# Retention and soft mixture of experts: the first result write on eight DMA engines

## The chip, the cores and the metric

The kernel runs on one core of a Trainium2 chip. The time is the device time of one execution in microseconds (us), the median of 3 runs. Times inside an execution are counted from the start of the profiled span.

## The reference

First a linear attention with decay. For each of 4 batches and 8 heads, 768 steps of a 64 x 64 state:

```
state = gamma[head] * state + outer(k[t], v[t])
y[t]  = scale * q[t] @ state            # scale = 1/sqrt(64)
```

The outputs of the heads stand side by side as x, 3072 tokens of 512 columns (one row for each batch and step). Then a soft mixture of 8 experts with 4 slots each:

```
logits = x @ phi                        # 3072 x 32
slot_in  = softmax(logits, over tokens).T @ x          # 32 x 512
slot_out[e] = relu(slot_in[e] @ w1[e]) @ w2[e]         # w1: 512 x 1024, w2: 1024 x 512
out = softmax(logits, over slots) @ slot_out           # 3072 x 512
```

All of it is float32.

## The kernel before, in words

The order of all instructions on each engine is written out by hand: the order of the statements is the order on the engine, and nothing is planned by a scheduler. All transfers, loads and writes alike, are issued by SyncE (SP), in one queue.

The attention is worked in chunks of 128 steps, two chunks at a time, and the tokens' logits and the sums for the slots are gathered along the way. Meanwhile the weights w1 and w2 come in, in loads of 2 MB (`load_two`, issued on line 177). The last four of these loads hold the last parts of w2.

After the attention come the experts: `hidden` (line 678) multiplies the slots by w1, the loop of line 766 multiplies the result by w2. The 512 output columns are worked in three blocks (`BLOCKS`) of 256, 128 and 128 columns. Each block ends in the generator `finish`, whose steps are fitted between the matmuls of the following block: at each `yield` it hands back to the loop over units of the next block, which goes on with one unit of its matmuls.

In `finish` the expert outputs of the block are spread over the partitions (line 729), and then for each 64 columns of the block's width there is one unit `u` (line 733): four matmuls (line 742), one for each batch, make 128 output columns (on partitions) for 1536 of the 3072 tokens (on the free axis, three chunks of 128 of each batch). ScalarE and VectorE copy the four results of PSUM into the tile `ot` (line 750), and SP writes the tile to `out` (line 753). The output in DRAM is turned, 512 rows (columns of the model) of 3072 tokens, so a write of 128 rows by 1536 tokens is 768 KB in pieces of 6144 bytes, with 12288 bytes from row to row. The host turns it back.

In order there are eleven writes, numbered here one to eleven. Block 0 has four of 768 KB (its units 0 to 3). Block 1 has one of 768 KB, and from `HELD` on a unit is written in two halves of 384 KB, so that two more follow in block 1 and four in block 2. Write one, with rows 0 to 127 and the first 1536 tokens, is the one that the change touches. The first unit of block 0 has the number `(cb, u) == (0, 0)` and is written in one part.

After the last write the core waits for all writes to land (line 841), and the execution ends.

Of the kernel before, what the change touches and what calls it, by code (L numbers as in the profile page):

```python
# [16 lines left out]
B, H, S, D = 4, 8, 768, 64  # L17
C = 128
NC = S // C
NSTEP = B * NC  # L20
NPAIR = H // 2
NTOK = B * S
DM = H * D
# [3 lines left out]
NK = DM // 128  # L27
NFC = FF // 128
HC = C // 2
NPP = NSTEP // 2  # L30
WARM = 4
WM = 1
# [19 lines left out]
MOVES.update({P: [(P - 1, 0, MIX), (P - 1, 1, MIX)] for P in range(3, 8)})  # L52
WITHK = [[i for i in (2 * P, 2 * P + 1) if i not in TURNED and i < NSTEP - B] for P in range(NPP)]
ROWS = [[P for P in range(1, NPP - B // 2) if len(WITHK[P]) == n] for n in range(3)]
KINDS = [n for n in range(3) if ROWS[n]]
# [10 lines left out]
def head_of(half, g):  # L66
    return 2 * g + np.where(g < NPAIR // 2, half, 1 - half)


def constants():  # L70
# [4 lines left out]
    k[:, K_VC:K_VC + H] = g[None, :] ** -float(C)  # L75
    gy = g[head_of(p[:, None] // HC, np.arange(NPAIR)[None, :])]
    k[:, K_YT:K_YT + 64] = (gy[:, :, None] ** (8 * np.arange(16)) / np.sqrt(D)).reshape(128, 64)
# [7 lines left out]
def retention_soft_moe_kernel(  # L85
# [4 lines left out]
    nc = tc.nc  # L90
    xs = dict(zip(KINDS, arrays))
    xw, wone, wtwo, whalf, wl, kq, head, v1, out = arrays[len(KINDS):]
# [12 lines left out]
    def large(pool, n=4096):  # L105
        return pool.tile([128, n], F32, name="b", tag="b")

    def slot():
        return ring.tile([128, 1024], F32, name="r", tag="r")

    def small(name, shape, bufs=1):
        return cpool.tile(shape, F32, name=name, bufs=bufs)

    def bank(name, shape=(128, 512)):
        return ps.tile(list(shape), F32, name=name)
# [27 lines left out]
    def half(r):  # L143
        return slice(r * HC, (r + 1) * HC)

# [51 lines left out]
    def load_behind(P):  # L197
        m = P - (NPP - B // 2)
        t = st[2 * P]["tile"][:, 0:3072]
        nc.sync.dma_start(t, wl[m])  # L200
        take(early[8 + 12 * m:20 + 12 * m], t)
# [4 lines left out]
    def load_pair(P):  # L206
# [9 lines left out]
        if P == 0:  # L216
# [4 lines left out]
            nc.sync.dma_start(t[:, 2560:3072], v1)  # L221
        elif P >= NPP - B // 2:
            m = P - (NPP - B // 2)
            nc.sync.dma_start(t, xw[m])
# [45 lines left out]
    def carry_mm(P):  # L270
        p = pr[P] = {}
        names = (("Y0", "Y1"), ("A1", "S")) if P == NPP - 1 else (("Y0", "Y1"),)
        p["Y"] = [bank(n).rearrange("p (i g t) -> p i g t", i=2, t=C) for pair in names for n in pair]
# [424 lines left out]
    for hf in range(2):  # L698
        for g2 in range(2):
# [14 lines left out]
                    hidden_t(0)  # L714
    assert not weights

    tags = [["sm", "A2", "A0", "A3", "S", "Y1", "Y0"], ["sm", "A2", "Y1", "A3", "S", "A1", "Y1", "A3"],
            ["sm", "A2", "A0", "Y0", "A1", "A3", "S", "Y1"]]
    pend = []

    def finish(cb, op):
        c0, w = BLOCKS[cb]
        os_ = small("os", [128, 256])
        s4 = slot()
        nc.vector.tensor_copy(os_[:, :w], op[:, :w])
        for _ in range(Y1[cb] - 1):
            yield
        rp = bank("Y0")
        nc.tensor.matmul(rp[:, :w], rep, os_[:, :w], start=True, stop=True)
        nc.vector.tensor_copy(s4[:, :w], rp[:, :w])  # L730
        for _ in range(Y2[cb] - 1):
            yield
        for u in range(w // 64):
            m, h = divmod(u, 2)
            if h == 0:
                ots = large(big)
            ot = ots[:, 2048 * h:2048 * h + 12 * C]
            parts = 2 if (cb, u) >= HELD else 1
            cps = []
            for j in range(B):  # L740
                cp = bank(tags[cb][(B * u + j) % len(tags[cb])]).rearrange("p (c t) -> p c t", t=C)[:, 0:3]
                nc.tensor.matmul(cp, s4[32 * j:32 * j + 32, m * 128:(m + 1) * 128],  # L742
                                 cT[32 * j:32 * j + 32, 3 * h:3 * h + 3, :], start=True, stop=True,
                                 skip_group_check=True, tile_position=(32 * j, 0))
                cps.append(cp)
            if (cb, u) == HELD:
                yield
            for p in range(parts):
                for j in range(p * B // parts, (p + 1) * B // parts):
                    (nc.scalar.copy if j % 2 else nc.vector.tensor_copy)(  # L750
                        ot[:, j * 3 * C:(j + 1) * 3 * C].rearrange("p (c t) -> p c t", t=C), cps[j])
                n = 12 * C // parts
                nc.sync.dma_start(out[c0 + m * 128:c0 + (m + 1) * 128, h * 12 * C + p * n:h * 12 * C + (p + 1) * n],
                                  ot[:, p * n:(p + 1) * n])
                if (cb, u, p) == (*HELD, 0):
                    yield
            for _ in range(BURST[cb]):
                yield

    for cb, (c0, w) in enumerate(BLOCKS):  # L760
        op = bank(("A0", "A1")[cb % 2])
        units = ([(g, 4 * hf + f) for hf in range(2) for g in range(2) for f in range(4)] if cb == 0 else
                 [(g, fc) for g in range(2) for fc in range(NFC)])
        for n, (g, fc) in enumerate(units):
            for j in range(4):
                nc.tensor.matmul(op[32 * j:32 * j + 32, :w], hT[fc // 4][:, fc % 4, 4 * g + j, :],  # L766
                                 w2t[4 * g + j, cb, fc], start=(n == 0), stop=(n == len(units) - 1),
                                 skip_group_check=True, tile_position=(0, 32 * j))
            if cb == 0 and n == 2:
                hidden_t(1)  # L770
            for f in pend:
                next(f, None)
        done = finish(cb, op)
        next(done)
        if cb == len(BLOCKS) - 1:
            next(pend[0])
            next(pend[0])
            next(done)
        for f in pend:
            for _ in f:  # L780
                pass
        pend = [done]
# [41 lines left out]
                head=np.concatenate([constants(), phi.reshape(128, NPAIR * NSLOT), vn[0]], axis=1), v1=vn[1])  # L824


_OUT = (DM, NTOK)


# [16 lines left out]
```

## Time and profile before

| | us |
|---|---|
| median of 3 runs (148.18 to 148.61) | 148.55 |
| the profiled execution | 148.68 |
| its span in the profile | 147.0 |
| TensorE busy (matmul) | 136.7 (93%) |
| VectorE busy | 92.5 (63%) |
| ScalarE busy | 77.9 (53%) |
| GpSimd busy | 73.2 (50%) |

The span is the stretch from the first to the last instruction in the profile; the execution's own time is 1.7 us longer. 59.2 MB are moved in 6792 packets, at a mean of 403 GB/s; 52.56 MB are read from DRAM and 6.29 MB written. The core has 16 DMA engines, and a share of DMA time in the views is the mean over these 16: a share of 0.5 can be eight engines that work all the time. The profile does not tell the engines apart by number. A transfer has landed when its last engine is done, and "issue to landing" counts from the start of the instruction on SP to then.

### The profile page before, as it was taken

The numbers are of one execution on the slowest core, as the hardware profiler recorded it, in microseconds if no ns is written. First come the engines' busy times: TensorE is split into PE (matmuls) and PEld (weight loads), VectorE is DVE, ScalarE is ACT, GpSimd is POOL, SyncE is SP. The second block draws the span as 40 slices with busy tenths as digits, with TensorE's granted clock in tenths as the row PEclk, the third lists the DMA queues.
The fourth block names the chain that finished last, engine by engine and source line by source line (L and its number), as shares of the span: only waits on it lengthen the run. The fifth ranks groups of instructions, "written<-read, shape, count | busy, mean of one in ns | idle before, by whom it ended". The sixth has DMA issues, their size and how long they took to land.

```text
span 147.0 us, 5562 instructions
## 1 busy us (share of the span) xinstructions
PE 136.7 (93%) x2378; PEld 101.5 (69%) x2378; DVE 92.5 (63%) x199; ACT 77.9 (53%) x196; POOL 73.2 (50%) x139
## 2 busy tenths in 40 slices
PE   7999999999999999999999989999999999989800
PEld 2678989997999799978988868864333466557400
DVE  0386847977988898979897999486320202563530
ACT  3082496798679875989485795650510100442320
POOL 2035499999979897888693998901100000000000
PEclk9999999999999999999999999999999999999996
DMA  4999999999999999999999999999999999899894
GB/s 169 355 409 422 435 423 436 409 446 416 417 424 404 439 425 430 425 416 436 424 428 424 428 419 417 415 420 409 419 441 430 428 428 419 350 389 380 343 397 168
DMA packets 6792, 59.20 MB, mean 403 GB/s; under 512 B 752, under 2 KB 752, under 8 KB 3440
## 3 DMA queue, kind: packets, MB, share of 16 engines
q1 hardware_dynamic: 6768, 58.85, 96.0%
q8 instruction: 18, 0.29, 0.8%
q14 instruction: 6, 0.05, 0.1%
HBM read 52.56 MB, written 6.29 MB: 400 GB/s over the span
## 4 chain that ended last, share of the span: by engine, by line
PE 82%; DVE 7%; DMA 4%; issue 1%; SPq 1%; DVEq 0%; POOL 0%
PE Y L292 15%; PE A L259 14%; PE A L766 9%; PE S L321 6%; PE Y L283 6%; PE Y L678 5%; PE A L678 5%; PE A L235 5%; DMA r<-in_head_dram 4%; PE sm L375 3%; PE Y L431 2%; DVE b L750 2%; PE sm L742 2%; DVE r L267 2%; PE Y L235 1%; PE S L742 1%
## 5 line engine op out<-in xcount | busy, mean ns | idle before, releaser
L358 ACT COPY r<-r 32x256 f32<-32x256 f32 x96 | 38.6, 402 | 5.7 <-DVE r L348 4.7
L267 DVE TENSOR_TENSOR r<-A,mi 128x512 f32<-128x512 f32 (+1 forms) x50 | 30.1, 661 | 11.7 <-PE A L259 11.7
L358 POOL COPY r<-r 32x256 f32<-32x256 f32 x64 | 25.2, 393 | 6.0 <-DVE r L348 2.0
L259 PE MATMUL A<-b 64*128 64x128 f32 x384 | 25.2, 279 | 0.3 <-DMA b<-in_kq_dram 0.2
L259 PEld LDWEIGHTS A<-b 64*128 64x128 f32 x384 | 22.6, 188 | 3.5 <-issue 1.5
L248 POOL TENSOR_TENSOR b<-b,kt 128x512 f32<-128x512 f32 x22 | 22.5, 1043 | 2.4 <-ACT kt L508 2.0
L292 PE MATMUL Y<-r,b 128*64 128x128 f32 x352 | 22.5, 276 | 0.7 <-DVE r L267 0.5
L292 PEld LDWEIGHTS Y<-r,b 128*64 128x64 f32 x352 | 19.2, 137 | 3.1 <-issue 1.2
L241 POOL TENSOR_TENSOR b<-b,qtab 128x256 f32<-128x256 f32 x20 | 14.3, 738 | 6.9 <-DMA b<-in_x_dram 4.4
L766 PE MATMUL A<-b,r 128*32 128x128 f32 (+1 forms) x368 | 15.7, 307 | 0.0
L766 PEld LDWEIGHTS A<-b,r 128*32 128x32 f32 x368 | 10.6, 110 | 5.8 <-issue 3.8
L750 ACT COPY b<-A 128x384 f32<-128x384 f32 x10 | 4.5, 483 | 16.8 <-PE A L742 15.2
L348 DVE STREAM_TRANSPOSE r<-r 128x1024 f32<-128x1024 f32 x10 | 12.4, 1237 | 0.0
L283 PE MATMUL Y<-b,sst 64*64 64x128 f32 x304 | 10.6, 276 | 0.0
L321 PE MATMUL S<-b 128*64 128x64 f32 x304 | 10.5, 222 | 0.0
L321 PEld LDWEIGHTS S<-b 128*64 128x64 f32 x304 | 10.2, 138 | 0.0
L236 ACT COPY b<-A 128x512 f32<-128x512 f32 x13 | 7.2, 588 | 4.4 <-PE A L235 4.0
L283 PEld LDWEIGHTS Y<-b,sst 64*64 64x64 f32 x304 | 8.2, 133 | 1.3 <-issue 0.2
L312 DVE TENSOR_TENSOR r<-Y,qtab 128x512 f32<-128x512 f32 x9 | 6.2, 692 | 4.2 <-PE Y L292 4.2
L235 PE MATMUL A<-mi,b 128*128 128x128 f32 x52 | 7.6, 281 | 0.0
L375 PEld LDWEIGHTS sm<-r,kt 128*32 128x32 f32 x192 | 5.3, 110 | 2.8 <-issue 2.7
L678 PE MATMUL A<-b,qtab 128*32 128x512 f32 x64 | 7.1, 594 | 0.0
(159 smaller groups left out, 189.5 us busy)
## 6 DMA issues: line engine op xcount, KB each, us to landing
b<-in_wtwo_dram SPq DMA_DIRECT2D x12, 2048.0 KB, 16.1
b<-in_x_dram SPq DMA_DIRECT2D x8, 1536.0 KB, 10.7
b<-in_xw_dram SPq DMA_DIRECT2D x2, 2048.0 KB, 14.5
out_dram<-b SPq DMA_DIRECT2D x5, 768.0 KB, 6.6
b<-in_wl_dram SPq DMA_DIRECT2D x2, 1536.0 KB, 11.5
out_dram<-b SPq DMA_DIRECT2D x6, 384.0 KB, 3.9
b<-in_wone_dram SPq DMA_DIRECT2D x2, 1024.0 KB, 12.1
b<-in_x_dram SPq DMA_DIRECT2D x2, 768.0 KB, 8.3
```

The costliest lines, as they stand in the source:

```text
L235: nc.tensor.transpose(kp[:, g * 128:(g + 1) * 128], st[i]["kT"][:, g, :], ident)
L241: nc.gpsimd.tensor_tensor(q[:, 0:2], q[:, 0:2], qtab[:, 0:2], ALU.mult)
L248: nc.gpsimd.tensor_tensor(v, v, vsc[:, a:b].unsqueeze(2).broadcast_to([128, b - a, D]), ALU.mult)
L259: nc.tensor.matmul(s["sc"][r][:, g, :], s["kT"][half(r), g, :], s["qT"][half(r), g, :], start=True, stop=True, skip_group_check=True)
L267: nc.vector.tensor_tensor(s["A"][:, r, g:g + n], s["sc"][r][:, g:g + n], mask.unsqueeze(1).broadcast_to([128, n, C]), ALU.mult)
L283: nc.tensor.matmul(p["y"][k][b][half(half_of(r, g)), gl, :], sst[(2 * P + k) % B][half(r), g, :], s["qT"][half(r), g, :], start=(gl == 0 a ...
L292: nc.tensor.matmul(pr[P]["y"][k][g // 2][half(half_of(r, g)), g % 2, :], s["v"][:, 2 * g + r, :], s["A"][:, r, g, :], start=(P < B // 2 an ...
L321: nc.tensor.matmul(S_[half(r), k, g, :], s["kn"][:, 2 * g + r, :], s["v"][:, 2 * g + r, :], start=True, stop=True, skip_group_check=True)
L348: nc.vector.transpose(x, pr[P]["yT"].rearrange("p i g t -> p (i g t)"))
L358: {"s": nc.scalar.copy, "g": nc.gpsimd.tensor_copy}[on[n % len(on)]](xn[32 * b:32 * b + 32, :, a], x[32 * a:32 * a + 32, :, b])
L678: nc.tensor.matmul(hp[hf][32 * j:32 * j + 32, :], si0[:, a:a + NSLOT], w1t[hf, g, k][j], start=(g == 0 and k == 0), stop=(g == 1 and k == ...
L766: nc.tensor.matmul(op[32 * j:32 * j + 32, :w], hT[fc // 4][:, fc % 4, 4 * g + j, :], w2t[4 * g + j, cb, fc], start=(n == 0), stop=(n == le ...
```

## The change

Write one is no longer one transfer of 128 partitions into rows 0 to 127 of `out`. It is four transfers of 32 partitions each (`q` from 0 to 3), 192 KB, into an area of DRAM behind the 512 rows. This area (`gaps`) has 4 x 8 x 5 rows of 1536 elements. Each transfer fills, in each of eight blocks of five rows, the first four rows; the fifth stays empty. Within a block the four rows of 6144 bytes follow each other without space. The output tensor has 80 more rows of 3072 for it. On the host the area's rows are copied to their place before the output is turned.

The `continue` ends the unit's only part. It passes a `yield` that belongs to another unit, `HELD`. The other ten writes are as before.

```
+GAP = (4, 8, 5)
...
+    gaps = out[DM:].rearrange("r t -> (r t)").rearrange("(q a b t) -> q a b t", q=GAP[0], a=GAP[1], b=GAP[2])
...
                 n = 12 * C // parts
+                if (cb, u) == (0, 0):
+                    for q in range(GAP[0]):
+                        nc.sync.dma_start(gaps[q, :, 0:GAP[2] - 1], ot[32 * q:32 * q + 32, 0:n])
+                    continue
                 nc.sync.dma_start(out[c0 + m * 128:c0 + (m + 1) * 128, h * 12 * C + p * n:h * 12 * C + (p + 1) * n],
                                   ot[:, p * n:(p + 1) * n])
...
-_OUT = (DM, NTOK)
+_OUT = (DM + int(np.prod(GAP)) // 2, NTOK)
...
-    o = np.asarray(r.results[0]["out_0_dram"]).reshape(DM, 2, B, NC // 2, C)
+    o = np.array(r.results[0]["out_0_dram"])
+    o[0:C, 0:NTOK // 2] = o[DM:].reshape(*GAP, NTOK // 2)[:, :, 0:-1].reshape(C, NTOK // 2)
+    o = o[0:DM].reshape(DM, 2, B, NC // 2, C)
```

## Rows read from the trace of the kernel before

**Rows 1.** The page: engines' busy time, DMA queues, the chain's share by engine.

```profile
PE 136.7 (93%) x2378; PEld 101.5 (69%) x2378; DVE 92.5 (63%) x199; ACT 77.9 (53%) x196; POOL 73.2 (50%) x139
...
q1 hardware_dynamic: 6768, 58.85, 96.0%
q8 instruction: 18, 0.29, 0.8%
...
PE 82%; DVE 7%; DMA 4%; issue 1%; SPq 1%; DVEq 0%; POOL 0%
```

**Rows 2.** Chain of waits, its last piece: start, length, what.

```profile
140.54 0.47 DVE b L750
```

**Rows 3.** SP's queue in order of time: last load; writes one, two, four, five, eleven.

```profile
108.40 0.33 SPq L177 DMA_DIRECT2D b<-in_wtwo_dram  x1
...
126.74 0.35 SPq L753 DMA_DIRECT2D out_dram<-b  x1
128.39 0.34 SPq L753 DMA_DIRECT2D out_dram<-b  x1
...
131.70 0.33 SPq L753 DMA_DIRECT2D out_dram<-b  x1
135.82 0.33 SPq L753 DMA_DIRECT2D out_dram<-b  x1
...
141.43 0.91 SPq L753 DMA_DIRECT2D out_dram<-b  x1
```

**Rows 4.** Issue to landing, one transfer each: last load; writes four, five, six, eleven.

```profile
DMA to landing us min/median/max: 22.9/22.9/22.9
...
DMA to landing us min/median/max: 6.9/6.9/6.9
DMA to landing us min/median/max: 4.6/4.6/4.6
DMA to landing us min/median/max: 3.5/3.5/3.5
...
DMA to landing us min/median/max: 4.7/4.7/4.7
```

**Rows 5.** Stretches from write one to the end; last columns: PE clock, DMA share, GB/s.

```profile
126.75:127.50 0.75, 0.75 (x20) 0.29 (x16) 0.20 (x1) 0.15 (x1) 0.00 (x0) 1.00 0.51 218
...
130.00:132.00 2.00, 1.81 (x48) 1.09 (x41) 1.22 (x3) 0.86 (x2) 0.00 (x0) 1.00 1.00 412
135.00:135.25 0.25, 0.25 (x16) 0.25 (x12) 0.25 (x1) 0.24 (x1) 0.00 (x0) 1.00 0.68 270
135.25:135.50 0.25, 0.25 (x20) 0.25 (x16) 0.11 (x1) 0.00 (x0) 0.00 (x0) 1.00 0.53 221
135.75:136.00 0.25, 0.25 (x18) 0.25 (x12) 0.00 (x0) 0.00 (x0) 0.00 (x0) 1.00 0.59 246
136.25:136.50 0.25, 0.25 (x12) 0.15 (x8) 0.01 (x1) 0.00 (x0) 0.00 (x0) 1.00 0.43 156
142.00:144.00 2.00, 0.00 (x0) 0.00 (x0) 0.00 (x0) 0.00 (x0) 0.00 (x0) 1.00 1.01 401
144.75:145.00 0.25, 0.00 (x0) 0.00 (x0) 0.00 (x0) 0.00 (x0) 0.00 (x0) 0.50 0.20 74
...
145.25:145.50 0.25, 0.00 (x0) 0.00 (x0) 0.00 (x0) 0.00 (x0) 0.00 (x0) 0.50 0.09 37
145.50:145.75 0.25, 0.00 (x0) 0.00 (x0) 0.00 (x0) 0.00 (x0) 0.00 (x0) 0.50 0.06 25
```

**Rows 6.** DMA packets begun in 127.57:127.65, 136.63:136.72 and 136.72:136.81 (writes: under 8 KB).

```profile
DMA packets 7, 0.05 MB, mean 666 GB/s; under 512 B 0, under 2 KB 0, under 8 KB 6
...
DMA packets 8, 0.05 MB, mean 546 GB/s; under 512 B 0, under 2 KB 0, under 8 KB 8
DMA packets 5, 0.03 MB, mean 341 GB/s; under 512 B 0, under 2 KB 0, under 8 KB 5
```

**Rows 7.** SP's queue: two loads issued one behind the other.

```profile
94.60 0.90 SPq L188 DMA_DIRECT2D r<-in_whalf_dram  x2
```

## The prediction

> **What bounds the kernel now.** I read the page's totals first, then the chain of waits, then the end stretch by stretch, since the change touches one write in the last seventh of the span. TensorE is busy 93% of the span and holds 82% of the chain, while the transfers that SP issues take 96% of sixteen DMA engines' time [rows 1]. Both are full; the question is which of them sets the last microseconds. The chain's last piece is a VectorE copy at 140.54 to 141.01 [rows 2], after which no engine computes; the last write is issued at 141.43 [rows 3] and lands 4.7 us later, at 146.1 [rows 4]. The span is 147.0, so 0.9 us of closing waits follow the landing. From 141.0 on the time is thus DMA time alone.
>
> What the reader should see there is that the sixteen DMA engines do not end together. The windows' DMA share times 16 is the number of engines at work. In 142 to 144 it is 1.01: all of them. From 144.75 to 145.00 it is 0.20, three engines; from 145.25 to 145.50 0.09, one to two; up to 145.75 0.06, one [rows 5]. So thirteen engines end near 144.75 and three end 0.4 to 1.0 us later, and these three set the time.
>
> They are late since the loads. The last load of weights is issued at 108.40 [rows 3] and lands 22.9 us later [rows 4], at 131.3, but already in 126.75 to 127.50 the share is 0.51 [rows 5]: eight engines have finished it and stand idle, eight are still reading, up to 4 us longer. A cause fits in size: the instruction fetches, 18 packets of 16 KB in 0.8% of sixteen engines' 147 us [rows 1], are 0.008 x 16 x 147 = 18.8 us, about 1.05 us for each fetch on one engine; eight late engines with two or three fetches each are late by about what is seen. The first write is issued at 126.74 [rows 3], so it finds eight engines free and eight with a backlog; six packets of its size start between 127.57 and 127.65 [rows 6], some 0.85 us after the issue.
>
> **The change part by part.** *The moved bytes.* 768 KB on sixteen engines are 48 KB each. All sixteen move 412 GB/s in 130 to 132 [rows 5], 25.8 GB/s for one, so 48 KB take 1.9 us. On eight engines each has 96 KB, 3.8 us: eight engines gain 1.9 us of work and eight lose 1.9 us. The total is the same; only who does it changes.
>
> *The relieved eight,* if these are the late ones. Between write four and write five there is a pause: write five is issued at 135.82 [rows 3] and its data start some 0.85 us later, near 136.7: of thirteen packets of its size, eight begin between 136.63 and 136.72 and five up to 136.81 [rows 6]. Write four, issued at 131.70 [rows 3], lands 6.9 us later [rows 4], at 138.6; 1.9 us earlier it would land at 136.7, its engine being done 0.35 us before that (the last write's engine ends at 145.75 and lands at 146.1), so before write five starts. All late engines would catch up there, and the floor of the end is that of the thirteen: 1.0 us earlier.
>
> *The loaded eight,* if these are the early ones. Their pause before write five pays for the extra work, and no more than that. The share falls to 0.68 in 135.00 to 135.25, 0.53 in the next quarter, 0.59 in 135.75 to 136.00 and 0.43 in 136.25 to 136.50 [rows 5]: five engines are free at about 135.1, seven to eight by 135.5, and the last of the eight perhaps by 136. Their pause up to 136.7 is 1.6 us for the first and 0.7 us or less for the last, against 1.9 us of extra work. So they begin write five 0.3 us late at best and about 1.2 us late at worst. How much of a lateness survives to the end is read from today's late engines: write five lands 4.6 us after its issue [rows 4], at 140.4, where an engine with no backlog would need 0.85 + 1.9 + 0.35 for the landing, 138.9; they are 1.5 us late there and 1.0 us at the end, so some 0.5 us is made up. A lateness of 0.3 to 1.2 us becomes 0 to 0.7, or up to 1.2 if none is made up. Against the 1.0 us of today the gain is 0.2 us less than nothing to 1.0 us; the last of the eight decides, since one engine is enough to hold the end. I take 0.65 us late at the end, a gain of 0.35, nearest to the row of 136.25 to 136.50, where the last of them comes free.
>
> *The three added issues.* Two loads issued one behind the other take 0.90 us of SP's queue [rows 7], 0.45 us each, so four issues run from 126.74 to about 128.5. Write two, issued at 128.39, slips by 0.1 to 0.2 us. Nothing but later writes is queued behind it on SP, and every engine has work until then or later: the early eight to 131.4 with the doubled write, the late eight with loads to 129 and more; so I cost it at nothing, and at 0.2 us for the relieved engines if that cover fails, which their pause before write five absorbs. The `continue` passes no yield (the one behind it is for another unit), so TensorE's order stays. The copies before the write are unchanged. Three more completions on an engine cannot gain; above they are bounded by what write six's landing of 3.5 us [rows 4] has over 0.85 + 0.95 + 0.35 us, 1.35, nearly all of it backlog of the write before; I take nothing. The gap in DRAM moves no bytes, and no row before shows a write of this row order; I bound it at 10% of 3.8 us either way, -0.4 to +0.4 us, and take 0.
>
> [...]
>
> *Sum.* The profiled execution took 148.68 us, span 147.0 and 1.7 us around it; less 0.35 that is 148.33. The median of the runs is 148.55, which makes 148.2.
>
> **The rivals.** *The eight are the wrong ones.* The rows count engines but do not name them. If the new writes run on engines that are late, the last engine gets 1.9 us more with no pause to take it up (it works from the load to the end): 148.55 + 1.8 = 150.3 to 150.5. It decides as soon as one of the three late ones is among the eight. By the share alone it would be even odds. What speaks against it is the order of starts: on write five thirteen waiting engines begin over 0.18 us, eight of them in the first half; on write one, where only early engines wait, six begin in 0.08 us and none of them as late after the issue as the last five of write five [rows 6]. So the early engines look like those that are served first, the low end of the order, and a transfer cut to eight engines would most simply take these; it is indirect. [...] Chance 0.16.
>
> *It doesn't do what it says.* The four writes still go over all sixteen engines, or over engines chosen afresh for each: then bytes and engines are as before, only three issues more, 148.55, at most 0.2 above. Every transfer in this trace has 128 partitions, so none shows how blocks of eight are spread. Chance 0.09.
>
> *The early eight become the last.* Same mechanism as the forecast, but one slow engine of the eight keeps the full lateness of 1.0 us or more: 148.45 to 148.75, no change. This is the forecast's upper end and is counted with it.
>
> **How the numbers follow.** The forecast, early eight loaded, has 0.75; its own range is 147.7 to 148.7. This kernel's runs can tell a change only beyond 0.3%, 0.45 us, that is below 148.1 or above 149.0. The forecast's gain lies between 0 and 0.9 around 0.35, so its 0.75 is split 0.37 faster, 0.33 same and 0.05 slower. Without effect 0.08 same, 0.01 slower; the wrong eight 0.16 slower. Together faster 0.37, same 0.41, slower 0.22. The range of 147.6 to 149.0 leaves out the wrong eight and little else.
>
> **What would show it.** In the changed trace: four issues of 192 KB from 126.7 to 128.5; the share in the end's quarters falling within 0.5 us instead of 1.0; write four landing in less than 6.9 us; the pause before write five gone for eight engines (share at 135.25 to 136.50 near 0.5 to 0.6, though from the other half); TensorE's times unchanged up to 141. Wrong if write one's parts land late (over 5 us for the first of them), which would mean that they queue behind the loads, or if the tail has engines that end 2 us after the rest.

## The result, and the profile after

The changed kernel takes 149.99 us (median of 6 runs, 149.16 to 150.91) against 148.56 us (6 runs, 148.18 to 148.62) for the kernel before: the ratio is 1.01, with a 95% interval of 1.0061 to 1.014. It is slower by 1.4 us, where 0.35 us of gain were forecast. The profiled execution took 149.87 us with a span of 148.2, so 1.19 us more than that of before. All ratios are taken from undisturbed runs alone and are not ratios of the medians, which take in every run; where the two differ the ratio counts.

From the page of the changed kernel: busy times, DMA queues, the chain's shares by engine. They answer to [rows 1].

```profile
PE 137.2 (93%) x2378; PEld 102.0 (69%) x2378; DVE 92.3 (62%) x199; ACT 77.9 (53%) x196; POOL 73.4 (50%) x139
...
q1 hardware_dynamic: 6784, 58.85, 95.7%
q8 instruction: 18, 0.29, 0.8%
...
PE 87%; DVE 4%; DMA 2%; issue 0%; DVEq 0%
```

The totals hardly move: same bytes, same matmuls. The 1.2 us are not in the totals but in which engine works when. The last VectorE copy of the changed kernel (start, length) is over at 140.59, 0.4 us earlier than [rows 2]; so the computation is not what got slower.

```profile
140.04 0.55 DVE L752 COPY b<-S 128x384 f32<-128x384 f32 x1
```

SP's queue of the changed kernel, start and length: last load, writes two, five and eleven, which answer to [rows 3]. Line 757 issues the four parts of write one, line 759 the other writes.

```profile
108.22 0.33 SPq L178 DMA_DIRECT2D b<-in_wtwo_dram  x1
...
129.66 0.36 SPq L759 DMA_DIRECT2D out_dram<-b  x1
...
135.01 0.33 SPq L759 DMA_DIRECT2D out_dram<-b  x1
...
142.23 0.73 SPq L759 DMA_DIRECT2D out_dram<-b  x1
```

The four parts by themselves, in the view of one source line (shortest, median and longest duration in ns, first and last start):

```profile
L757 SPq DMA_DIRECT2D out_dram<-b x4: 652/672/821, 126.6 to 128.9; - x4
```

One issue of this form takes 0.65 to 0.82 us where the one of before took 0.35 [rows 3]. Four of them hold SP from 126.56 to 129.54. The last load went out 0.18 us earlier than before, so without the change write two would have gone at 128.21; it goes at 129.66, 1.45 us late.

Issue to landing of writes four, five and eleven, against 6.9, 4.6 and 4.7 us in [rows 4]:

```profile
DMA to landing us min/median/max: 8.0/8.0/8.0
DMA to landing us min/median/max: 6.5/6.5/6.5
...
DMA to landing us min/median/max: 4.9/4.9/4.9
```

Did the parts run on the engines that were free? DMA packets begun between 127.85 and 128.10, some 1.4 us after the first issue (under 8 KB are writes):

```profile
DMA packets 10, 0.10 MB, mean 410 GB/s; under 512 B 0, under 2 KB 0, under 8 KB 6
```

Six writing packets begin together, while other engines still begin load packets. So six of the eight engines were free ones, as read from [rows 6].

The other two were not. The trace also records each count of a transfer's semaphore with its time: sixteen for each transfer of before, the last of them at the landing. Each of the four parts has nine. The first comes 1.1 to 1.2 us after the issue, for the first part before any data start; the other eight are read as the landings on eight engines, as sixteen counts go with sixteen engines. For the first part they fall at 129.25 to 129.32 on six engines and at 130.41 and 130.60 on the last two. These two began more than 1 us later: by its own counts the last load of weights reaches eight engines by 128.08 and the next ones only at 129.14, 129.33 and later.

The stretches of the changed kernel; the last two columns are the DMA share and GB/s. They answer to [rows 5].

```profile
126.50:131.50 5.00, 5.00 (x112) 2.84 (x104) 3.12 (x7) 2.58 (x6) 0.00 (x0) 1.00 0.68 252
...
129.50:130.00 0.50, 0.50 (x12) 0.29 (x8) 0.30 (x1) 0.18 (x1) 0.00 (x0) 1.00 0.46 123
130.00:130.50 0.50, 0.50 (x16) 0.16 (x12) 0.07 (x1) 0.03 (x1) 0.00 (x0) 1.00 0.48 197
...
131.50:132.00 0.50, 0.35 (x10) 0.24 (x2) 0.15 (x1) 0.00 (x0) 0.00 (x0) 1.00 1.38 295
...
135.00:137.50 2.50, 2.28 (x50) 1.34 (x38) 0.91 (x3) 0.58 (x2) 0.00 (x0) 1.00 1.03 410
...
145.00:145.25 0.25, 0.00 (x0) 0.00 (x0) 0.00 (x0) 0.00 (x0) 0.00 (x0) 0.50 0.91 356
145.25:145.50 0.25, 0.00 (x0) 0.00 (x0) 0.00 (x0) 0.00 (x0) 0.00 (x0) 0.50 0.58 234
...
146.50:146.75 0.25, 0.00 (x0) 0.00 (x0) 0.00 (x0) 0.00 (x0) 0.00 (x0) 0.50 0.09 37
146.75:147.00 0.25, 0.00 (x0) 0.00 (x0) 0.00 (x0) 0.00 (x0) 0.00 (x0) 0.50 0.00 0
```

The kernel before in two of these stretches, and its last full quarter:

```profile
126.50:131.50 5.00, 5.00 (x108) 2.97 (x112) 3.11 (x7) 2.63 (x7) 0.00 (x0) 1.00 0.92 377
...
135.00:137.50 2.50, 2.50 (x62) 1.76 (x54) 0.85 (x3) 0.40 (x2) 0.00 (x0) 1.00 0.70 280
...
144.50:144.75 0.25, 0.00 (x0) 0.00 (x0) 0.00 (x0) 0.00 (x0) 0.00 (x0) 0.50 0.84 320
```

Three things are to be seen. First, between 126.5 and 131.5 the share falls from 0.92 to 0.68: 0.24 x 16 x 5.0 = 19 engine-microseconds without work, 1.2 us for each engine. Around 130 half of the engines stand idle: most of the eight without a part of write one (the relieved ones) have finished their loads, and write two is not there yet. Second, the pause before write five, 0.30 x 16 x 2.5 = 12 engine-microseconds before, is gone for all sixteen, not for eight. Third, the end: the first engines finish about 0.5 us later (the share is 0.91 up to 145.25, before 0.84 up to 144.75), and the last one 1.0 us later (146.75 against 145.75). The spread of the end, 1.0 us before, has become 1.5 us. Such ends are those of one execution each, and executions of one kernel differ by some 0.5 us and more, so a spread is a sign and not a price.

### The profile page after: what moved, and what is told of

Same layout as the page of the kernel before. It is cut to its first block, busy times and chain, and to the rows that moved or that the text cites. A ratio compares the mean times of both kernels' runs of the same rounds, so it can differ in the third digit from the quotient of the medians.

```text
span 148.2 us, 5565 instructions
## 1 busy us (share of the span) xinstructions
PE 137.2 (93%) x2378; PEld 102.0 (69%) x2378; DVE 92.3 (62%) x199; ACT 77.9 (53%) x196; POOL 73.4 (50%) x139
## 4 chain that ended last, share of the span: by engine, by line
PE 87%; DVE 4%; DMA 2%; issue 0%; DVEq 0%
PE A L260 17%; PE Y L293 14%; PE A L772 9%; PE S L322 6%; PE Y L284 6%; PE Y L679 5%; PE A L679 5%; PE A L236 5%; PE sm L376 4%; PE Y L432 3%; DMA b<-in_kq_dram 2%; DVE b L752 2%; PE sm L744 2%; DVE r L268 2%; PE Y L236 1%; PE S L744 1%
## 5 line engine op out<-in xcount | busy, mean ns | idle before, releaser
L260 PE MATMUL A<-b 64*128 64x128 f32 x384 | 25.7, 282 | 0.1
```

Source lines behind the costliest of these rows:

```text
L260: nc.tensor.matmul(s["sc"][r][:, g, :], s["kT"][half(r), g, :], s["qT"][half(r), g, :], start=True, stop=True, skip_group_check=True)
```

## The experiments

Three theories were set against each other. A: the four long issues hold SP, write two goes late, and the relieved engines idle. B: eight engines read partitions that other engines read at the same time for the next write, and the two slow each other's packets (an assumption of the author: no trace shows which engine reads which partitions). C: the loaded engines carry 1.9 us more than their pause before write five pays for, and the end waits for the last of them. The kernel before ran beside each batch, at 148.49 to 148.69 us. The diffs are against the changed kernel.

**Order of issue.** Write two goes first, the parts of write one behind it.

```
-                    for q in range(GAP[0]):
-                        nc.sync.dma_start(gaps[q, :, 0:GAP[2] - 1], ot[32 * q:32 * q + 32, 0:n])
                     continue
...
+                if (cb, u) == (0, 1):
+                    for q in range(GAP[0]):
+                        nc.sync.dma_start(gaps[q, :, 0:GAP[2] - 1], ots[32 * q:32 * q + 32, 0:n])
```

> Write two is issued first, and the four parts of write one behind it; bytes and engines as in the changed kernel. Theory A (the four issues hold SP's queue for 3 us, so that write two is issued 1.4 us late and the relieved eight stand idle from 129.3 to 130.8): write two goes out at about 128.2, its packets on the relieved eight start at 129.1, no idle stretch, and the time falls by 1 us or more, to 148.3 to 149.0. Theory C (the loaded eight simply have 1.9 us more than their pause pays for): the same 150.0. Theory B (two engines read from the same partitions' side and both slow down): in between, 149.3 to 149.8, since the parts still meet another write.

Measured: 151.06 us, ratio 1.0137 (1.0073 to 1.02). No better. Its stretch of 132 to 133 shows where the idle time went:

```profile
132.00:133.00 1.00, 1.00 (x20) 0.39 (x16) 0.00 (x0) 0.00 (x0) 0.00 (x0) 1.00 0.45 172
```

Now it is write three, issued at 131.37 behind the four parts, for which half of the engines wait. Moving the hold does not remove it.

**Four plain writes.** Four issues of 32 partitions, but to the old rows, meant for all sixteen engines.

```
-                        nc.sync.dma_start(gaps[q, :, 0:GAP[2] - 1], ot[32 * q:32 * q + 32, 0:n])
+                        nc.sync.dma_start(out[32 * q:32 * q + 32, 0:n], ot[32 * q:32 * q + 32, 0:n])
```

> Write one as four writes of 32 partitions to its old rows, without blocks and gaps, so that sixteen engines should move each. Tells the number of issues from the eight engines. If an issue costs 0.35 to 0.45 us here, write two slips by 0.2 us at most and the time is that of before, 148.5 to 148.8: then the 0.65 to 0.82 us of an issue in the changed kernel come from the eight engines. If each issue takes 0.65 us or more here too, the count alone holds the queue and the time is 149.0 to 149.6.

Measured: 149.0 us, ratio 1.0023 (1.0002 to 1.0044). The four issues:

```profile
L757 SPq DMA_DIRECT2D out_dram<-b x4: 361/418/1604, 125.7 to 127.1; - x4
```

Three of them take 0.36 to 0.43 us, so the 0.65 to 0.82 us of the change belong to its form and not to the number of issues. But the fourth takes 1.60 us, and write two goes out as late as in the change, at 128.84 after a first part at 125.75 (3.1 us). It costs 0.3 us: a late write two is cheap here, where the engines have work meanwhile (a DMA share of 0.93 between 126.5 and 131.5, against 0.68 in the change).

**One write on eight engines.** All 128 partitions in one issue, in eight blocks.

```
-GAP = (4, 8, 5)
+GAP = (1, 8, 17)
...
-                    for q in range(GAP[0]):
-                        nc.sync.dma_start(gaps[q, :, 0:GAP[2] - 1], ot[32 * q:32 * q + 32, 0:n])
+                    nc.sync.dma_start(gaps[0, :, 0:GAP[2] - 1], ot[:, 0:n])
```

> Write one as one write of 128 partitions whose rows in DRAM stand in eight blocks of sixteen with gaps: eight engines, one issue. Theory A: SP is held for under 1 us, write two goes out by 128.2 to 128.4, and the time is 148.2 to 148.8, at or under before. Theory C: 149.8 to 150.2 as in the changed kernel, since the same engines get the same bytes. Theory B: 149 to 150, since the engines read partitions that other engines read for write two.

Measured: 153.52 us, ratio 1.0313 (1.0266 to 1.036), with a single issue of 0.77 us. The slowest of all has the shortest hold of those with eight blocks, so A alone can't explain the loss. (That it uses eight engines like the parts of the change is assumed from its form.) Its stretch of 130 to 131 has a full share at a low rate:

```profile
130.00:131.00 1.00, 1.00 (x19) 0.40 (x16) 0.37 (x2) 0.25 (x1) 0.00 (x0) 1.00 0.91 276
```

0.91 of sixteen engines' time is taken, but 276 GB/s are moved where [rows 5] has 412 at 1.00: packets here take longer for the same bytes, as B expects. That shared partitions are the cause no run shows.

**Write one left out.** The four parts are not issued at all; their rows of the output are missing.

```
-                    for q in range(GAP[0]):
-                        nc.sync.dma_start(gaps[q, :, 0:GAP[2] - 1], ot[32 * q:32 * q + 32, 0:n])
                     continue
```

> Write one is left out, all else as before: no bytes of it on any engine. It gives the most that relieving the late engines can bring. If the end is set by three engines with a backlog since the loads, 147.5 to 147.8 (1.0 us or less under before, the span between thirteen and the last engine). If the backlog has little to do with it, 148.2 or more.

Measured: 148.28 us, ratio 0.9967 (0.9944 to 0.999). This bounds the whole idea: with write one costing nothing to anybody, the kernel gains 0.5 us by the ratio and 0.3 by the median, not the 1.0 us of the prediction's floor.

**Halves.** Only the parts with partitions 0 to 63 are written, or only those with 64 to 127; the rest of write one is left out.

```
-                    for q in range(GAP[0]):
+                    for q in (0, 1):
```

> Of the four parts of write one only the first two go out (partitions 0 to 63); partitions 64 to 127 are left out. [...] Theory A (hold of SP's queue): two issues of 0.7 us, write two 0.7 to 0.9 us late, 148.4 to 148.9. Theory C (0.95 us more on eight engines, inside their pause): 148.2 to 148.5. [...]

```
-                    for q in range(GAP[0]):
+                    for q in (2, 3):
```

> The same with the last two parts only (partitions 64 to 127); partitions 0 to 63 are left out. Same issues, bytes and engines as with the lower half. Theories A and C: the same time as the lower half within 0.3 us. Theory B: packets of 450 ns and more between 129 and 132, and 0.4 us or more above the lower half, 148.8 to 149.6.

Measured: 148.38 us, ratio 0.9967 (0.9937 to 0.9997), and 148.15 us, ratio 0.9971 (0.9946 to 0.9996). Both are as fast as with no write at all: the eight carry the 48 KB each that they carried before, and the others none. But the upper half's packets are slow; its stretch of 129.5 to 130:

```profile
129.50:130.00 0.50, 0.50 (x12) 0.31 (x8) 0.43 (x1) 0.31 (x1) 0.00 (x0) 1.00 1.46 315
```

A share above 1 at 315 GB/s: packets overlap and take longer for their bytes. The slow packets that B expects are there, and with half the load they cost nothing that the runs can tell.

**Lower half twice.** The load and the issues of the change, but all parts read partitions 0 to 63, so no packet comes from the upper ones (the upper half's data are not written).

```
-                        nc.sync.dma_start(gaps[q, :, 0:GAP[2] - 1], ot[32 * q:32 * q + 32, 0:n])
+                        nc.sync.dma_start(gaps[q, :, 0:GAP[2] - 1], ot[32 * (q % 2):32 * (q % 2) + 32, 0:n])
```

> Four issues on eight engines as in the changed kernel, but parts three and four read partitions 0 to 63 again in place of 64 to 127. Bytes, issues, engines and rows in DRAM as in the changed kernel. Theories A and C: 150.0 as the changed kernel, within 0.4. Theory B: no packets over 300 ns between 131 and 132, DMA rate of 400 GB/s there instead of 295 to 320, and 149.3 or less.

Measured: 149.99 us, ratio 1.0088 (1.0067 to 1.011): the whole loss without the slow packets of the upper half. Its stretches:

```profile
126.50:131.50 5.00, 5.00 (x112) 2.84 (x104) 3.15 (x7) 2.58 (x6) 0.00 (x0) 1.00 0.68 277
...
144.50:144.75 0.25, 0.00 (x0) 0.00 (x0) 0.00 (x0) 0.00 (x0) 0.00 (x0) 0.50 0.74 295
...
146.75:147.00 0.25, 0.00 (x0) 0.00 (x0) 0.00 (x0) 0.00 (x0) 0.00 (x0) 0.50 0.06 25
```

Without slow packets the first engines end near 144.7, as before, but the last one at 147.0: the spread grows to 2.3 us. The total is that of the change all the same: what the first engines gain, the last ones lose.

**At the pause.** Write one is plain again; write five goes in four parts of the new form instead, when most engines are free.

```
-                if (cb, u) == (0, 0):
+                if (cb, u) == (1, 0):
...
-    o[0:C, 0:NTOK // 2] = o[DM:].reshape(*GAP, NTOK // 2)[:, :, 0:-1].reshape(C, NTOK // 2)
+    o[256:256 + C, 0:NTOK // 2] = o[DM:].reshape(*GAP, NTOK // 2)[:, :, 0:-1].reshape(C, NTOK // 2)
```

> Write one as before; instead write five, issued when most engines are idle, goes out as four parts on eight engines. Shows what an issue costs when the queues are empty. If 0.65 to 0.85 us are the price of an issue of this form, all four take that here too; if it is a wait for full queues, the first ones take 0.35 to 0.45 us. The time: eight engines get 1.9 us more with no pause behind it, 150.0 to 150.8 by theory C alone; 151 or more if shared partitions slow the upper parts too.

Measured: 150.27 us, ratio 1.011 (1.0087 to 1.0133). The four issues and two of its stretches:

```profile
L757 SPq DMA_DIRECT2D out_dram<-b x4: 651/668/816, 135.6 to 137.9; - x4
```

```profile
136.50:137.00 0.50, 0.50 (x8) 0.00 (x0) 0.09 (x1) 0.00 (x0) 0.00 (x0) 1.00 0.23 74
...
138.00:139.00 1.00, 1.00 (x15) 0.64 (x16) 0.46 (x2) 0.10 (x2) 0.00 (x0) 1.00 0.53 160
```

A share near 0.53 while hardly anything else is in flight is eight engines (0.53 x 16 = 8.5), and each part again has eight landings: the form does confine these transfers to eight. The second issue runs from 136.50 to 137.17, while only a quarter of the engines work (0.23), and takes just as long. So the 0.65 to 0.82 us belong to the form and not to a full queue.

**The hold without the load.** Each part carries 128 columns of 1536; the rest of write one is left out.

```
-                        nc.sync.dma_start(gaps[q, :, 0:GAP[2] - 1], ot[32 * q:32 * q + 32, 0:n])
+                        nc.sync.dma_start(gaps[q, :, 0:GAP[2] - 1, 0:C], ot[32 * q:32 * q + 32, 0:C])
```

> The four writes keep their form, their place and their partitions, but each carries 128 columns of 1536 only (16 KB in place of 192 KB); the rest of write one is left out. This keeps SP's four issues (0.65 to 0.82 us each) and the lateness of write two (about 1.45 us) and takes the load off the eight. Theory A (the issues hold the queue, the relieved eight fall idle and that decides): 149.3 to 150.0, nearly that of the change. Theory C (the eight carry 1.9 us more than their pause pays for, and the last engine is one of them): the lateness of write two is covered by the pause before write five, so 148.1 to 148.5, like the kernel with write one left out (148.28).

Measured: 148.06 us, ratio 0.9963 (0.9934 to 0.9993). SP is held as in the change,

```profile
L757 SPq DMA_DIRECT2D out_dram<-b x4: 651/670/821, 125.0 to 127.3; - x4
```

and nothing is lost against leaving write one out. The hold alone is not the cause, as C expected. (The bytes it leaves out widen the pause that covers the hold, so this doesn't clear the hold where the bytes are there.)

**The load without the hold.** Two issues, each of 32 partitions by 3072 columns of a weight tile in place of write one's data. The expectation says 64 partitions for each; as written the two read partitions 0 to 63 together, so this run is no test of B.

```
-GAP = (4, 8, 5)
+GAP = (2, 8, 9)
...
+        wide.append(t)
...
-                        nc.sync.dma_start(gaps[q, :, 0:GAP[2] - 1], ot[32 * q:32 * q + 32, 0:n])
+                        nc.sync.dma_start(gaps[q, :, 0:GAP[2] - 1], wide[9][32 * q:32 * q + 32, 0:2 * n])
```

> Two issues in place of four: each takes 64 partitions by 3072 columns from a weight tile (the output is not write one's data), so each of the eight engines still gets 96 KB, in the same two halves of the partitions as the lower-half-twice kernel spreads them, with half the holding of SP's queue. Theory A: write two goes out about 0.7 us after the write of before instead of 1.45, and the time falls by half of the change's loss or more, to 149.0 to 149.4. Theory C: the eight have the same load and the time stays at 149.8 to 150.3. Theory B (two engines that read the same partitions' side slow each other): the second issue reads the upper 64 partitions as in the change, so its packets take 430 to 700 ns; as the runs so far show it alone costs nothing.

Measured: 149.46 us, ratio 1.0063 (1.0029 to 1.0097). The run isolates the load better than planned. Its data need no copy, so both issues go out at 120.7, long before write two, which is on time:

```profile
120.72 1.55 SPq L760 DMA_DIRECT2D out_dram<-b  x2
128.35 0.35 SPq L762 DMA_DIRECT2D out_dram<-b  x1
```

Its stretches:

```profile
126.50:131.50 5.00, 5.00 (x110) 2.97 (x112) 3.11 (x7) 2.60 (x7) 0.00 (x0) 1.00 0.91 376
...
135.00:137.50 2.50, 2.42 (x54) 1.49 (x43) 0.85 (x4) 0.44 (x2) 0.00 (x0) 1.00 0.82 333
...
144.25:144.50 0.25, 0.00 (x0) 0.00 (x0) 0.00 (x0) 0.00 (x0) 0.00 (x0) 0.50 0.80 307
...
146.00:146.25 0.25, 0.00 (x0) 0.00 (x0) 0.00 (x0) 0.00 (x0) 0.00 (x0) 0.50 0.03 12
```

No idle time (0.91 against 0.92), no late write two, and the kernel is still 0.9 us slower (0.0063 x 148.5; 0.4 to 1.4 by the interval). The first engines end some 0.2 us earlier than before, near 144.45, the last near 146.15: a spread of 1.7 us. This is C by itself. Issue to landing of write five, which was issued at 135.19:

```profile
DMA to landing us min/median/max: 5.7/5.7/5.7
```

The landings on the single engines show who comes last. Part one lands on five of the eight by 129.78, and on the other three at 130.88, 131.40 and 131.75. These three then have no pause at all: each further 48 KB takes them 1.7 to 1.9 us, through write four (138.19, 138.71, 139.04) to write five (140.02, 140.54, 140.88). At the end three engines stand last with the same distances, at 145.67, 146.18 and 146.52; the other thirteen have landed by 145.12.

**Half on eight, half plain.** The lower 64 partitions as two parts, the upper 64 as one plain write.

```
-GAP = (4, 8, 5)
+GAP = (2, 8, 5)
...
+                    nc.sync.dma_start(out[64:C, 0:n], ot[64:C, 0:n])
...
-    o[0:C, 0:NTOK // 2] = o[DM:].reshape(*GAP, NTOK // 2)[:, :, 0:-1].reshape(C, NTOK // 2)
+    o[0:64, 0:NTOK // 2] = o[DM:].reshape(*GAP, NTOK // 2)[:, :, 0:-1].reshape(64, NTOK // 2)
```

> Only the lower 64 partitions go over eight engines, in two issues; the upper 64 are one plain write on all sixteen. The eight get 72 KB instead of 48 (0.95 us more), the others 24 KB instead of 48. Theory C: half the extra load fits the eight's pause of 0.7 to 1.6 us for most of them, so the time is between before and the change, 148.3 to 149.0. Theory A: three issues of .82, .65 and about .4 us, write two about 1.0 us late: 149.3 to 149.7. Theory B: no packet of the upper half is slow, so all of B's share of the loss goes: 148.3 to 148.8.

Measured: 149.65 us, ratio 1.0051 (1.0024 to 1.0078). Half the extra load (72 KB on each of the eight, if the plain half is spread evenly over sixteen) costs about half the loss; that is somewhat more than C forecast from the pause. A's forecast fits the time, though write two was only 0.6 us late (128.39, that is 2.28 us after the first part, where [rows 3] has 1.65 between writes one and two). So neither dose of the extra load gains, and which theory it speaks for stays open.

**Upper half first.** The four parts in reversed order.

```
-                    for q in range(GAP[0]):
+                    for q in reversed(range(GAP[0])):
```

> The four writes in reversed order, the upper partitions first. Load, issues and bytes are those of the change. Theories A and C: 149.7 to 150.3, no difference from the change. Theory B: the slow packets fall into the time when only six to eight engines work, and the first parts land later (about 2 us each instead of 1.1) while the last go at full pace; the time moves by 0.3 us or more, to either side.

Measured: 150.83 us, ratio 1.0141 (1.0091 to 1.0191), an interval that overlaps with that of the change. Whether the order matters stays unclear.

**A longer pause.** The change with write three left out, and the kernel before with the same write left out, so that every engine's pause is some 1.9 us longer (48 KB at 25.8 GB/s, a sixteenth of the 412 in [rows 5]). The same edit in both:

```
+                if (cb, u) == (0, 2):
+                    continue
                 nc.sync.dma_start(out[c0 + m * 128:c0 + (m + 1) * 128, h * 12 * C + p * n:h * 12 * C + (p + 1) * n],
```

> The change with write three (768 KB on all sixteen engines, 1.9 us of each) left out, so every engine's pause before write five is 1.9 us longer. Theory C (the pause is too short for 1.9 us more): now it suffices, the loaded eight begin write five with the others, and the late write two is covered as well: 148.0 to 148.5, within 0.3 us of the kernel before with the same write left out. Rival (the eight lose time that no pause pays, after write five too): 149.2 to 149.9, 1 us or more above it.

> The kernel before with write three left out, to stand beside the change with write three left out. All late engines catch up before write five, as with write one left out (148.28): 148.0 to 148.4 by either theory.

Measured: the change 0.9962 (0.9934 to 0.9991) of the kernel before, that of before 0.9976 (0.9953 to 0.9998). The difference of 1% that the change makes is gone. The change's stretches with the longer pause:

```profile
126.50:131.50 5.00, 4.84 (x109) 3.06 (x106) 3.26 (x7) 2.58 (x6) 0.00 (x0) 1.00 0.79 284
...
143.50:143.75 0.25, 0.00 (x0) 0.00 (x0) 0.00 (x0) 0.00 (x0) 0.00 (x0) 0.50 1.04 406
...
144.00:144.25 0.25, 0.00 (x0) 0.00 (x0) 0.00 (x0) 0.00 (x0) 0.00 (x0) 0.50 0.19 74
144.25:144.50 0.25, 0.00 (x0) 0.00 (x0) 0.00 (x0) 0.00 (x0) 0.00 (x0) 0.50 0.00 0
```

The four long issues, the slow packets and the eight loaded engines are all there; only the pause is longer. The engines end within 0.5 us (1.04 up to 143.75, none after 144.25). This profiled execution took 147.39 us, 1.2 less than the median of its kernel (148.56; 148.26 for the other), so the ratios carry more than its end does. By their intervals, some 0.5 us either way between the two, a long enough pause pays for what the change adds, and the loss is a matter of the pause.

**Two issues at the place.** The load and partitions of the kernel that writes the lower half twice, in two issues that read their 32 partitions twice (the upper half's data are not written).

```
-GAP = (4, 8, 5)
+GAP = (2, 8, 9)
...
-                        nc.sync.dma_start(gaps[q, :, 0:GAP[2] - 1], ot[32 * q:32 * q + 32, 0:n])
+                        src = ot[32 * q:32 * q + 32, 0:n].unsqueeze(1).broadcast_to([32, 2, n])
+                        nc.sync.dma_start(gaps[q, :, 0:GAP[2] - 1], src)
```

> The bytes, engines and partitions of the kernel that writes the lower half twice (each of the eight gets 96 KB, no packets from the upper partitions), at write one's place, but in two issues that read their 32 partitions twice, so SP is held some 1.5 us instead of 3.0 (the upper 64 rows of write one's block get no data of their own). Theory A for the rest of the loss (the holding adds to the load's price): write two at about 128.3 to 128.5, little idle time of the relieved eight, 149.3 to 149.7. Theory C alone: 149.8 to 150.2, as with four issues.

Measured: 150.09 us, ratio 1.0075 (1.0045 to 1.0105). Write two is on time (128.33) and the loss is that of four issues. Its end:

```profile
144.25:144.50 0.25, 0.00 (x0) 0.00 (x0) 0.00 (x0) 0.00 (x0) 0.00 (x0) 0.50 0.78 307
...
147.25:147.50 0.25, 0.00 (x0) 0.00 (x0) 0.00 (x0) 0.00 (x0) 0.00 (x0) 0.50 0.06 25
```

The first engines end near 144.45, the last one at 147.5 or later: 3 us of spread, in an execution of 150.86 us that is 0.8 us above the median. With the hold halved the whole loss is in the late engines.

## Why the prediction was wrong

*The mechanism* was half right. The form takes eight engines (eight landings for each part), six of them in the change were free ones, the bytes and the computation stay as they were, and the pause before write five is what has to pay. That blocks of eight would confine a write to eight engines was shown by no row of before, though the sum rests on it; the changed kernel's eight landings for each part showed it, and a share of 0.53 at the pause agrees.

*The step that failed* is the condition of the loaded eight, "if these are the early ones". It was put at 0.75 and gave all eight a pause of 1.6 to 0.7 us. Not all of the eight are early: two of them in the change and three in the kernel with the load alone were still reading weights when the others began, and the three had no pause at all. The pause of the early ones was read well. In the prediction's reckoning an engine without backlog lands write five 3.1 us after its issue, and the loaded ones were to be 0.3 to 1.2 us late there. With the load alone, where write five could land at 138.29, the five early ones of the eight are at most 1.1 us late (139.37), and at most 0.4 behind the first engine at the end. The three others are 1.7 to 2.6 us late there, and they are the last at the end. (In the change the two late ones stand out less: the last part lands on them at 133.16 and 133.35, on the six at 132.73 to 132.96, and slow packets and fetches, below, lie over the rest.) So the term "0.65 us late at the end" measured 1.7 us with the load alone and 1.5 in the change, where the last engine lands write five 3.4 us late (6.5 against 3.1), against 1.0 at the end of before: a loss, instead of a gain of 0.35. The kernel's time says the same, 0.9 and 1.4 us more. The rival of the wrong eight, with a chance of 0.16, was thus right for two or three of the eight; its price of 150.3 to 150.5 is a little above the 149.99 measured.

The prediction had a row that warned of it: it read eight free engines from a share of 0.51, where [rows 6] shows six packets beginning together. And that a share counts engines without naming them it said itself.

*Instruction fetches* may widen the end in both kernels. One falls into the stretch before write five; DMA queues of the kernel before in 135.3 to 137.0,

```profile
q8 instruction: 1, 0.02, 3.6%
```

and of the changed one in 135.7 to 137.1 (queue, packets, MB, share):

```profile
q8 instruction: 1, 0.02, 4.2%
```

Each takes about 1.0 us of one engine (0.042 x 16 x 1.4 is 0.94). In the kernel before, a packet of write four ends at 136.11, the fetch begins just there, and the packet behind it takes 627 ns where 234 are usual: the engine lands write four at 138.40. It is one of the three that are late from write four on, so these were not all "late since the loads". In the change the fetch begins at 136.09, again followed by a packet of 627 ns, and a smaller one of 8 KB at 135.80. Two engines land write four there at 139.58 and 139.75, the others by 138.82, and two stand last at the end, at 147.12 and 147.17, the others by 146.32. So in the change's own profile the last 0.8 us fit fetches that fell on engines without a pause, and the load by itself fits the seven engines that end 0.3 to 0.8 us behind the first seven. Which engine a fetch hits is inferred from the times of the packets; no run took a fetch away.

*The floor,* a gain of 1.0 us, was not reached even with write one left out: 0.3 to 0.5 us. In that trace the engines do land within 0.4 us of each other (145.34 to 145.74), as the floor supposed. But by then fifteen of them have waited for write six, which is issued at 138.24 there and at 137.92 in the kernel before. An even end is no earlier than the copies let the last six writes go out.

*The three added issues* were costed at nothing, with a slip of 0.1 to 0.2 us. The slip is 1.45 us: an issue of this form takes 0.65 to 0.82 us, not 0.45. The cover named for it was wrong too: the relieved engines did run dry, before write two came. By itself this costs nothing (0.9963 with small parts) or 0.3 us (1.0023 in the plain form). In the change the idle time of 19 engine-microseconds is more than the 12 of the pause, and the first engines end 0.5 us later. But the idle time doesn't explain that: the lower half written twice has the same share of 0.68, and its first engines end as before. What the change has beyond it is the slow packets. Write two lands on the first eight engines at 133.94 to 134.04 in the change and at 133.36 to 133.45 there.

*How they add up.* In the profile of the change 0.5 us is in the first engines' end and 0.5 in the spread. In the kernels without the slow packets the first is gone and the spread is larger, for about the same total: 1.0063 (load alone), 1.0075 (two issues) and 1.0088 (lower half twice) against 1.01, with intervals that overlap. So the load alone suffices for most of the loss. Whether the hold and the slow packets add anything to it in the change, the runs can't tell.

*The shared rows* (B) stood nowhere in the sum; the 0.4 us around 0 were for the order of the rows in DRAM. That order costs nothing to be seen: the lower half twice moves 277 GB/s at a share of 0.68, the kernel before 377 at 0.92, which is the same for each engine at work. The packets of the upper half are slower, up to 1.38 of share for 295 GB/s, but the time shows none of it where the load is halved. The one write in eight blocks loses 4.65 us (0.0313 x 148.56), of which the load explains some 0.9; the rest goes with slow packets (276 GB/s at a share of 0.91), which no run took out of that kernel. That shared partitions make them slow was not shown.

*What would show it.* The issues ran to 129.54 instead of 128.5; write four landed after 8.0 us, not under 6.9; the end spread over 1.5 us, not 0.5; the pause was gone for sixteen and not eight. The last copy came 0.4 us early, otherwise TensorE's times came as said. The two signs of being wrong did not show: the first part landed after 4.0 us, not over 5, and the tail was 1.5 us, not 2. Every kernel with the full load in eight blocks and the pause of before is 0.6 to 3.1% slower, and the four plain writes 0.2%.

## What to carry to other kernels

Here an idle stretch evened out uneven engines, and it could be spent only once: with the pause of before the change lost 1%, with one some 1.9 us longer the difference was gone. Before work is put on the engines that seem free, find out which engines it will use: a share counts free engines and does not name them, while the landings of a trial transfer, one for each engine, tell how many of its engines were late. Then compare the extra time with the shortest pause among these, not with the mean. Test the most that an idea can bring by leaving the work out; here that one run would have shown 0.3 to 0.5 us, against the 1.4 us that were lost. And take the price of an issue from a run of its own form: four issues held SP for 3.0 us, in the new form and in the plain one, where one had taken 0.35.

## What the runs showed of the hardware

An issue on SP of a transfer in eight blocks took 0.65 to 0.85 us, with loads queued before it (load alone, at 120.7) as with three quarters of the engines idle (at the pause), and up to 1.25 with the upper half first. That of a plain write took 0.33 to 0.43, and up to 1.6 with several writes in flight. In the trace of the change each part has one count ahead of its eight landings, 1.1 to 1.2 us after the issue, and each write of before has sixteen counts. No run here shows what writes the count ahead, or whether it is the added time.

Packets of the eight engines took the usual time (234 ns for 6144 bytes) when the data lay in partitions 0 to 63 (233 to 236 ns in the change between 127 and 129), and longer when they lay in 64 to 127: the share rose to 1.46 at 315 GB/s with the upper half alone, and the change has packets of up to 701 ns between 131 and 132. The lower half twice moves more in the same stretch (277 against 252 GB/s at the same share of 0.68). With one issue for all 128 partitions 0.91 of the share moved 276 GB/s, and that kernel was the slowest, by 3.1%.
